# The second layer of a routed expert block by one level of Strassen's scheme, in half-width column tiles

## The chip, the cores and the metric

The kernel runs on one core of one Trainium2 chip. The metric is the device time of one execution in microseconds; before the change the median of three runs is 424.77 us (424.56 to 424.95). The profile is one further execution, with a span of 419.8 us. The five engines of a core are called here as in the profile: PE (TensorE, matrix products; PEld is its weight load), DVE (VectorE), ACT (ScalarE), POOL (GpSimd) and SP (SyncE, which issues most transfers).

## The reference, cut to what matters

Two stages. The first is a linear attention with a decaying state; it gives a matrix x of 3072 tokens by 384. The second sends each token to one of 8 experts. Everything is in 32-bit floats.

```python
# first stage, per batch and head
y[t]  = r[t] @ (state + outer(u * k[t], v[t]))
state = w[:, None] * state + outer(k[t], v[t])

# second stage: N = 3072 tokens, D = 384, E = 8 experts, F = 1024
logits     = x @ w_gate
expert_idx = argmax(logits, axis=1)
gate_w     = softmax(logits)[arange(N), expert_idx]
for e in range(E):
    mask = expert_idx == e
    h  = maximum(x[mask] @ w1[e], 0.0)      # first layer,  384 -> 1024
    ye = h @ w2[e]                          # second layer, 1024 -> 384
    out[mask] = gate_w[mask, None] * ye
```

## The kernel before

The attention half and the routing take about the first 157 us of the span. Then the tokens stand in tiles of 128, all of one expert, and a loop works through the tiles. Two tiles run ahead of the loop, the loop has 22. A tile gathers its tokens from HBM with an indirect transfer (`load_x`), transposes them (`turn`), and applies the first layer (`hidden`, in two halves of four blocks of 128 hidden units each) and the second layer (`result`). Which expert a tile has is only known at run time, so instructions that read the weights `w2_all` take an index from a register.

```python
def turn(self, mo, tag, copy=nc.vector.tensor_copy):
    p = self.R.ps.tile([128, DT, 128], FP32, name="xTp", tag=tag, bufs=BUFS[tag])
    for d in range(DT):                                   # DT = 3
        nc.tensor.transpose(p[:, d, :], self.xs[:, 128 * d:128 * d + 128], ident)
    self.xT = self.tile(mo, [128, DT, 128], "xT", 2)
    copy(self.xT, p)

def hidden(self, mo, fb):
    if fb == 0:
        self.hT = self.tile(mo, [128, FT, 128], "hT", 2)  # FT = 8
    p = self.R.ps.tile([128, 4, 128], FP32, name="hp", tag=f"P{fb}", bufs=2)
    for f in range(4):
        q, o = 2 * fb + f // 2, f % 2 * 128
        for d in range(DT):
            nc.tensor.matmul(p[:, f, :], lhsT=self.w1[:, q, d, o:o + 128], rhs=self.xT[:, d, :],
                             start=d == 0, stop=d == DT - 1)                      # L1045
    nc.scalar.activation(self.hT[:, 4 * fb:4 * fb + 4, :], p, func=ACT.Relu)      # L1047

def result(self, mo, within=None):
    p = self.R.ps.tile([128, DM], FP32, name="yp", tag="y", bufs=2)               # DM = 384
    e = slice(self.j, self.j + 1) if self.early else ds(self.expert(ENG.PE), 1)
    for f in range(FT):
        # ... cut: work of the next tile that one early tile puts in here
        rhs = w2_all[:, e, f * DM:(f + 1) * DM]
        nc.tensor.matmul(p, lhsT=self.hT[:, f, :], rhs=rhs, start=f == 0, stop=f == FT - 1)  # L1056
    self.y = self.tile(mo, [128, DM], "yo", 3)
    nc.vector.tensor_scalar_mul(self.y, p, self.xs[:, DM:W])                      # L1058
```

The loop (`tiles` are the 22; `seg` is one tile more that holds the remainders of four experts, 32 tokens each, whose work is spread over the loop in eight odd tiles):

```python
for j, t in enumerate(tiles):
    i = (j - 5) // 2 if j % 2 and 5 <= j < 5 + 4 * FQ else None    # FQ = 4
    if j + 2 < len(tiles):
        tiles[j + 2].load_x(mo)
    # ... cut
    t.hidden(mo, 0)
    if i is not None:
        if i < FQ:
            seg.quarter(mo, i)      # hg: 12 products in column tiles of 32
        else:
            seg.add(i - FQ)         # yg: 8 products in column tiles of 32
        if i + 2 < 2 * FQ:
            seg.load(mo, i + 2)
    t.hidden(mo, 1)
    if i is not None and i < FQ:
        seg.turn_quarter(i)         # hgT: two transposes
    if j + 2 < len(tiles):
        tiles[j + 2].load_w1(wp)
    # ... cut
    if j + 1 < len(tiles):
        tiles[j + 1].turn(mo, "g")
    # ... cut
    t.result(mo)
    t.store()
    # ... cut
```

The attention half holds instructions whose durations are of use here: pairs of products that write the two halves of 64 partitions (column tiles), lines L599 and L603, and elementwise products on GpSimd (L514, L515, L520) and VectorE (L510).

Of the kernel before, what the change touches and what calls it, by code (L numbers as in the profile page):

```python
# [10 lines left out]
FP32 = mybir.dt.float32  # L11
# [3 lines left out]
ALU = mybir.AluOpType  # L15
ACT = mybir.ActivationFunctionType
PSUM = bass.MemoryType.PSUM
ENG = mybir.EngineType

B, H, S, D = 4, 8, 768, 48  # L20
E, F = 8, 1024
DM = H * D
# [7 lines left out]
DT = DM // 128  # L30
FT = F // 128
WLO, WHI = 0.6, 1.6
W = DM + 1
SEG = 32
NS = 4
# [3 lines left out]
FQ = 4  # L39
FW = F // FQ  # L40
# [13 lines left out]
def rwkv5_then_switch(ctx, tc, r, k, v, rk, tok, wu_in, wg, wgh, w1, w2, out):  # L54
# [8 lines left out]
    nc = tc.nc  # L63
# [6 lines left out]
    w2_all = consts.tile([128, E, FT * DM], FP32, name="w2_all")  # L70
# [62 lines left out]
    with tc.manual_schedule():  # L133
# [10 lines left out]
        for l in range(LV):  # L144
            n = 1 << l
# [279 lines left out]
    def fast():  # L425
# [242 lines left out]
        for i, load in enumerate(pieces[AHEAD:]):  # L668
            piece.setdefault(turns[i * len(turns) // n], []).append(load)

        with tc.manual_schedule():
# [4 lines left out]
            for load in pieces[:AHEAD]:  # L676
                load()
# [18 lines left out]
            for u in range(NU):  # L696
# [4 lines left out]
                for load in piece.get(u, ()):  # L701
                    load()
# [53 lines left out]
            for step in R.onehots(B - 1):  # L756
# [13 lines left out]
            t1.store()  # L770
            late = late_tiles_of(R, NSURE - NEARLY)
            run_tiles(tiles[2:], wp, mo, Segments(R, 0), zip(late, [xbs[1][:, i] for i in range(G)] + [t0.xs, t1.xs],
                                                             strict=True))
        em.close()
# [213 lines left out]
    class Tile:  # L988
# [47 lines left out]
        def hidden(self, mo, fb):  # L1036


            if fb == 0:
                self.hT = self.tile(mo, [128, FT, 128], "hT", 2)  # L1040
            p = self.R.ps.tile([128, 4, 128], FP32, name="hp", tag=f"P{fb}", bufs=2)
            for f in range(4):
                q, o = 2 * fb + f // 2, f % 2 * 128
# [6 lines that stand above are left out]
            p = self.R.ps.tile([128, DM], FP32, name="yp", tag="y", bufs=2)  # L1050
            e = slice(self.j, self.j + 1) if self.early else ds(self.expert(ENG.PE), 1)
            for f in range(FT):
                if within and f == FT - 2:
                    within()
                rhs = w2_all[:, e, f * DM:(f + 1) * DM]
                nc.tensor.matmul(p, lhsT=self.hT[:, f, :], rhs=rhs, start=f == 0, stop=f == FT - 1)  # L1056
            self.y = self.tile(mo, [128, DM], "yo", 3)
            nc.vector.tensor_scalar_mul(self.y, p, self.xs[:, DM:W])  # L1058

        def store(self):  # L1060
            s_ = nc.gpsimd.indirect_dma_start(  # L1061
                out=out[:, :], out_offset=bass.IndirectOffsetOnAxis(ap=self.idx, axis=0),
                in_=self.y[:, :], in_offset=None, bounds_check=N - 1, oob_is_err=False)
            tc.declare_no_dep(s_.ins, group="sc", reason="each token stands in one tile: the rows are disjoint")
            tc.add_to_no_dep_group("sc", s_.ins)

    class Segments(Tile):
# [9 lines left out]
        def load(self, mo, i):  # L1077

            q = i % FQ
            if i == 0:  # L1080
                self.es = [self.expert(ENG.SP, NTILE + self.j * NS + k) for k in range(NS)]
                self.w = {}
            self.w[i] = self.tile(mo, [128, NS, DT * FW], "wq", 2)
            for k, e in enumerate(self.es):
                src = w1[ds(e, 1), q].rearrange("a p d f -> p (a d f)") if i < FQ else \
                    w2[ds(e, 1), q].rearrange("a p f -> p (a f)")
                nc.sync.dma_start(self.w[i][:, k], src)
# [26 lines left out]
        def add(self, q):  # L1114

            if q == 0:
                self.p = self.R.ps.tile([128, DM], FP32, name="yg", tag="rw", bufs=1)
            n = FT // FQ
            for f in range(n):
                for i in range(NS):  # L1120
                    t = slice(SEG * i, SEG * i + SEG)
                    nc.tensor.matmul(self.p[t, :], lhsT=self.hT[:, n * q + f, t],  # L1122
                                     rhs=self.w[FQ + q][:, i, f * DM:(f + 1) * DM], start=q == 0 and f == 0,
                                     stop=q == FQ - 1 and f == n - 1, skip_group_check=True)
# [5 lines left out]
    def run_tiles(tiles, wp, mo, seg, late):  # L1130


        for j, t in enumerate(tiles):
            i = (j - 5) // 2 if j % 2 and 5 <= j < 5 + 4 * FQ else None
            if j + 2 < len(tiles):
                tiles[j + 2].load_x(mo)
            if j == 2:
                seg.load_x(mo)
            t.hidden(mo, 0)
            if i is not None:  # L1140
                if i < FQ:
                    seg.quarter(mo, i)
                else:
                    seg.add(i - FQ)
                if i + 2 < 2 * FQ:
                    seg.load(mo, i + 2)
            t.hidden(mo, 1)
            if i is not None and i < FQ:
                seg.turn_quarter(i)
            if j + 2 < len(tiles):  # L1150
                tiles[j + 2].load_w1(wp)
            if j in (2, 3):
                seg.load(mo, j - 2)
            if j + 1 < len(tiles):
                tiles[j + 1].turn(mo, "g")
            if j == 4:
                seg.turn(mo, "rw")
            t.result(mo)
            t.store()
            if j >= 6:  # L1160
                for x, xs in islice(late, 1):
                    x.load_x(xs)
            if i == 2 * FQ - 1:
                seg.result(mo)
                seg.store()
# [31 lines left out]
    def after_general():  # L1197
        es, em = ExitStack(), ExitStack()
        ps = es.enter_context(tc.tile_pool(name="pm", bufs=1, space=PSUM))
        rt = es.enter_context(tc.tile_pool(name="rt", bufs=1))  # L1200
        mo = em.enter_context(tc.tile_pool(name="mo", bufs=2))
        R = Routes(ps, rt, 0)
        R.begin()
        for b in range(B):
            for step in R.ranks(b, "rw") + R.onehots(b):
                step()
        R.bases(rt)
        R.order(rt)
        R.owners(rt, NSURE)
        R.slots(rt)  # L1210
        R.index(rt, "rw")
        tiles = [Tile(R, j) for j in range(NSURE)]
        with tc.manual_schedule():
            for i in range(2):
                tiles[i].load_w1(mo)
                tiles[i].load_x(mo)
            tiles[0].turn(mo, "g")
            xl = rt.tile([128, NTILE - NSURE + E // NS - 1, W], FP32, name="xl")
            late = late_tiles_of(R, NSURE)
            run_tiles(tiles, mo, mo, Segments(R, 0), zip(late, [xl[:, i] for i in range(len(late))], strict=True))  # L1220
        em.close()
        late_tiles(R, late)
        es.close()
# [65 lines left out]
```

## Time and profile before

| | |
|---|---|
| median time | 424.77 us |
| span of the profiled execution | 419.8 us |
| PE busy, share of the span | 403.8 us, 96% |
| DVE, ACT, POOL busy | 153.2, 127.4, 150.2 us |
| granted PE clock, mean | 0.992 |
| first layer L1045, second layer L1056, share of the chain that ended last | 29%, 27% |
| transfers | 99.00 MB, mean 236 GB/s |

The page gives, for each engine, its busy time and how that lies over 40 slices of the span (a digit is tenths of a slice). The chain that ended last is found by going back from the last instruction, at each step to what released it. A timeline lists instructions in order of time; a run of equal instructions is merged into one row with its count. One 32-bit matrix product appears as two MATMUL and two LDWEIGHTS records, so counts of records are twice those of the code. In a timeline an instruction's releaser stands in brackets behind the idle time before it.

### The profile page before, as it was taken

To read this page: it belongs to the slowest core of one execution; us is meant where nothing else is said; L and a number is where in the kernel's file an instruction comes from. 1 tells how busy PE (TensorE), PEld (TensorE's weight loads), DVE (VectorE), ACT (ScalarE), POOL (GpSimd) and SP (SyncE) were. 2 spreads that over 40 slices of the span, in tenths; PEclk is the share of its full clock that TensorE was granted. 3 is DMA by queue.
4 is the path that set the end of the run, shared out by engine and by line. 5 is a ranking of instruction groups with operands and counts; after the bars stand their busy time and mean duration, and the time that the engine had idled before them with its cause. 6 is when DMAs were issued, how large, how long until landed. Compare 5 with 4: busy or idle time off the path is not lost.

```text
span 419.8 us, 10366 instructions
## 1 busy us (share of the span) xinstructions
PE 403.8 (96%) x4057; PEld 333.6 (79%) x4057; DVE 153.2 (36%) x409; ACT 127.4 (30%) x395; POOL 150.2 (36%) x192
## 2 busy tenths in 40 slices
PE   7999999999999979999999999999999999999990
PEld 7899999998999757788888777777878776776770
DVE  6887899999875910011111011110111011110100
ACT  4787777776773221111111011011111011011110
POOL 6998769569750021121111222122222111110100
PEclk9999999999999999999999999999999999999996
DMA  7989999999992999558866585976867675455000
GB/s 254 255 236 275 282 276 304 263 285 263 280 286 106 348 336 356 180 194 323 322 197 236 203 322 204 302 241 225 283 220 260 230 289 187 165 174 187 33 23 27
DMA packets 42944, 99.00 MB, mean 236 GB/s; under 512 B 5189, under 2 KB 16474, under 8 KB 42882
## 3 DMA queue, kind: packets, MB, share of 16 engines
q1 hardware_dynamic: 39024, 86.94, 63.7%
q0 software_dynamic: 3712, 11.23, 8.5%
q8 instruction: 37, 0.61, 0.7%
q14 instruction: 25, 0.20, 0.2%
q10 hardware_dynamic: 146, 0.01, 0.0%
HBM read 88.72 MB, written 9.65 MB: 234 GB/s over the span
## 4 chain that ended last, share of the span: by engine, by line
PE 86%; DVE 6%; ACT 2%; DMA 2%; POOL 1%; issue 1%; POOLq 0%; DVEq 0%
PE hp L1045 29%; PE yp L1056 27%; PE P L532 5%; PE P L542 5%; PE yp L603 5%; PE yp L599 4%; PE rp L634 4%; PE Gp L578 2%; PE xTp L1032 2%; DMA xs<-x_hbm,idx 1%; PE hg L1102 1%; PE yg L1122 1%; ACT A L553 1%; DVE At L842 1%; DVE A L564 1%
## 5 line engine op out<-in xcount | busy, mean ns | idle before, releaser
L1045 PEld LDWEIGHTS hp<-xT,w1s 128*128 128x128 f32 x1152 | 133.1, 192 | 10.4 <-issue 4.1
L1045 PE MATMUL hp<-xT,w1s 128*128 128x128 f32 x1152 | 135.2, 276 | 0.0
L1056 PE MATMUL yp<-w_all,hT 128*128 (+1 forms) x384 | 128.0, 486 | 0.0
L1056 PEld LDWEIGHTS yp<-w_all,hT 128*128 128x128 f32 x384 | 71.0, 190 | 44.3
L1047 ACT ACTIVATE hT<-hp 128x512 f32<-128x512 f32 x48 | 28.7, 598 | 225.5 <-PE hp L1045 185.4
L1061 POOL DMA_INDIRECT out_dram<-yo,idx x22 | 22.3, 1013 | 191.9 <-DVE yo L1058 182.4
L553 ACT ACTIVATE A<-ident,dv 128x128 f32<-128x128 f32 x192 | 59.7, 389 | 0.2 <-ACT dv L550 0.2
L1058 DVE TENSOR_SCALAR yo<-yp,xs 128x384 f32<-128x384 f32 x22 | 13.6, 618 | 106.5 <-PE yp L1056 106.5
L1034 DVE COPY xT<-xTp 128x384 f32<-128x384 f32 x23 | 12.8, 556 | 100.2 <-PE xTp L1032 100.2
L603 PE MATMUL yp<-A,w_all 128*64 128x128 f32 x384 | 39.7, 275 | 0.2
L514 POOL TENSOR_TENSOR w_all<-w_all 128x384 f32<-128x384 f32 x30 | 31.0, 1035 | 21.9 <-DMA w_all<-in_r_k_units_dram 5.4
L564 DVE COPY_PREDICATED A<-mask,P 128x384 f32<-128x384 int32 x64 | 36.2, 588 | 5.8 <-ACT A L553 5.2
L1026 POOL DMA_INDIRECT xs<-x_hbm,idx x22 | 21.3, 968 | 33.0 <-ACT idxs L986 26.6
L599 PE MATMUL yp<-w_all,St 128*64 128x128 f32 x320 | 32.6, 275 | 0.0
L515 POOL TENSOR_TENSOR w_all<-w_all,W 128x384 f32<-128x384 f32 x30 | 31.4, 1046 | 0.0
L542 PE MATMUL P<-w_all 48*128 48x128 f32 x384 | 29.5, 286 | 0.5 <-ACT dv L550 0.5
L532 PEld LDWEIGHTS P<-wu,w_all 48*128 48x128 f32 x384 | 23.9, 187 | 4.3 <-issue 1.9
L532 PE MATMUL P<-wu,w_all 48*128 48x1 f32 x384 | 26.7, 250 | 0.2 <-POOL St L449 0.2
L603 PEld LDWEIGHTS yp<-A,w_all 128*64 128x64 f32 x384 | 25.8, 137 | 1.3 <-DVE A L564 1.1
L520 POOL TENSOR_TENSOR Kg<-w_all,Wg 128x288 f32<-128x288 f32 (+1 forms) x32 | 25.5, 798 | 2.7 <-DVE Wg L474 2.1
L510 DVE TENSOR_TENSOR w_all<-w_all,W 128x384 f32<-128x384 f32 x30 | 25.9, 865 | 0.3 <-DMA w_all<-in_r_k_units_dram 0.3
L542 PEld LDWEIGHTS P<-w_all 48*128 48x128 f32 x384 | 24.2, 188 | 0.6 <-ACT dv L550 0.6
(167 smaller groups left out, 292.0 us busy)
## 6 DMA issues: line engine op xcount, KB each, us to landing
w1s<-in_moe_w_dram SPq DMA_DIRECT2D x22, 1536.0 KB
wq<-in_moe_w_dram SPq DMA_DIRECT2D x32, 384.0 KB
w_all<-in_v_k_units_dram SPq DMA_DIRECT2D x64, 144.0 KB
w_all<-in_r_k_units_dram SPq DMA_DIRECT2D x56, 144.0 KB
w_all<-in_moe_w_dram SPq DMA_DIRECT2D x20, 384.0 KB
w_all<-in_moe_w_dram SPq DMA_DIRECT2D x3, 1536.0 KB
x_hbm<-xb SPq DMA_DIRECT2D x9, 385.0 KB
w1s<-in_moe_w_dram SPq DMA_DIRECT2D x8, 384.0 KB
```

The lines of the kernel that those rows point to most:

```text
L510: nc.vector.tensor_tensor(x["R"], x["r"], bc(W1[:, x["hp"], None, :], [128, HC, C]), op=ALU.mult)
L514: nc.gpsimd.tensor_tensor(x["RK"], x["r"], x["k"], op=ALU.mult)
L515: nc.gpsimd.tensor_tensor(x["K"], x["k"], bc(W2[:, x["hp"], None, :], [128, HC, C]), op=ALU.mult)
L532: nc.tensor.matmul(P[hi][:, o:o + 1], lhsT=x["RK"][q, c, :], rhs=wu[q, 1, hp:hp + 1], start=True, stop=True, skip_group_check=True)
L542: nc.tensor.matmul(P[hi][:, c * C:(c + 1) * C], lhsT=x["K"][q, c, :], rhs=x["R"][q, c, :], start=True, stop=True, skip_group_check=True)
L553: nc.scalar.activation(A[:, hi, c, :], ident, func=ACT.Copy, scale=dv[:, hi, c:c + 1])
L564: nc.vector.copy_predicated(A[:, hi], bc(mask[:, None, :].bitcast(I32), [128, HC, C]), P[hi][:, 0:HC * C].rearrange("p (c t) -> p c t", t=C))
L599: nc.tensor.matmul(yp[q, c, :], lhsT=old[:, hi, :], rhs=x["R"][:, c, :], start=True, stop=False, skip_group_check=True)
L603: nc.tensor.matmul(yp[q, c, :], lhsT=vh(x, c, hi, 64), rhs=x["A"][:, hi, c, :], start=old is None, stop=True, skip_group_check=True)
L1045: nc.tensor.matmul(p[:, f, :], lhsT=self.w1[:, q, d, o:o + 128], rhs=self.xT[:, d, :], start=d == 0, stop=d == DT - 1)
L1047: nc.scalar.activation(self.hT[:, 4 * fb:4 * fb + 4, :], p, func=ACT.Relu)
L1056: nc.tensor.matmul(p, lhsT=self.hT[:, f, :], rhs=rhs, start=f == 0, stop=f == FT - 1)
```

## The change

Strassen's scheme multiplies two 2 x 2 block matrices with seven block products in place of eight, at the price of sums of blocks before and after. Here the tile's 128 tokens are cut into halves i of 64, the 1024 hidden units into halves of 512 (four blocks of 128 each), and the 384 output columns into halves of 192. A block product is then four products of a 64-column stationary operand with 192 moving columns. Since an output half has 64 tokens, it fills only half of the array's columns: two block products run side by side, one to partitions 0 to 63 and one to 64 to 127. The seventh is cut in two by its hidden units, and the two partial sums lie in the two halves. So there are 14 pairs of half products in place of 8 full ones, for 21 of the 22 tiles of the loop; the last tile and the two ahead of the loop keep `result`.

Sums of weight blocks (`T`, four) are formed for each tile anew, two on GpSimd and two on VectorE; sums of activation blocks (`S`, four) on VectorE; the seven products are put together by one ACT copy, eight VectorE adds and a scaling on ACT. To make room, `hT` and the segment weights `wq` have one buffer in place of two, and the segment loads stand later.

```diff
             if fb == 0:
-                self.hT = self.tile(mo, [128, FT, 128], "hT", 2)
+                self.hT = self.tile(mo, [128, FT, 128], "hT", 1)
...
+        def sums_w(self, mo, eng):
+            e = ds(self.expert(ENG.Pool if eng is nc.gpsimd else ENG.DVE), 1)
+            b = lambda i, k: w2_all[:, e].rearrange(
+                "p a (i f k d) -> p (a i) f k d", i=2, f=FT // 2, k=2)[:, i, :, k]
+            sub = lambda *a: eng.tensor_tensor(*a, op=ALU.subtract)
+            if eng is nc.gpsimd:
+                T = self.T = self.tile(mo, [128, 4, FT // 2, DM // 2], "T", 1)
+                sub(T[:, 3], b(1, 1), b(0, 1))
+                sub(T[:, 0], b(0, 1), b(0, 0))
+            else:
+                T = self.T
+                sub(T[:, 1], b(1, 1), T[:, 0])
+                sub(T[:, 2], b(1, 0), T[:, 1])
+
+        def sums_h(self, mo, fb):
+            a = lambda i, j: self.hT[:, FT // 2 * j:FT // 2 * j + FT // 2, 64 * i:64 * i + 64]
+            if fb == 0:
+                S_ = self.S = self.tile(mo, [128, 4, FT // 2, 64], "S", 1)
+                nc.vector.tensor_tensor(S_[:, 3], a(0, 0), a(1, 0), op=ALU.subtract)
+            else:
+                S_ = self.S
+                nc.vector.tensor_tensor(S_[:, 0], a(1, 0), a(1, 1), op=ALU.add)
+                nc.vector.tensor_tensor(S_[:, 1], S_[:, 0], a(0, 0), op=ALU.subtract)
+                nc.vector.tensor_tensor(S_[:, 2], a(0, 1), S_[:, 1], op=ALU.subtract)
+
+        def products(self):
...          # a, b, s, t: blocks of hT, w2, S, T
+            self.p = [self.R.ps.tile([128, 2, DM // 2], FP32, name=f"m{i}", tag="y", bufs=2) for i in range(2)]
+            def product(i, k, *halves):
+                for f in range(n):                                   # n = 4
+                    for hi, (x, y) in enumerate(halves):
+                        nc.tensor.matmul(self.p[i][64 * hi:64 * hi + 64, k, :], lhsT=x(f), rhs=y(f),
+                                         start=f == 0, stop=f == n - 1, skip_group_check=True)
+            product(0, 0, (a(0, 0), b(0, 0)), (a(1, 1), t(2)))
+            product(0, 1, (a(0, 1), b(1, 0)), (s(3), t(3)))
+            product(1, 0, (s(2), b(1, 1)), (s(0), t(0)))
+            for f in range(n // 2):
+                for hi in range(2):
+                    g = f + n // 2 * hi
+                    nc.tensor.matmul(self.p[1][64 * hi:64 * hi + 64, 1, :], lhsT=s(1)(g), rhs=t(1)(g),
+                                     start=f == 0, stop=f == n // 2 - 1, skip_group_check=True)
+
+        def combine(self, mo):
+            lo, up, k = slice(0, 64), slice(64, 128), DM // 2
+            p, q = self.p
+            u = self.tile(mo, [128, 3, k], "u", 1)
+            y = self.y = self.tile(mo, [128, DM], "yo", 3)
+            add = lambda *a: nc.vector.tensor_tensor(*a, op=ALU.add)
+            nc.scalar.copy(u[lo, 0], p[lo, 0])
+            add(y[lo, 0:k], p[lo, 1], u[lo, 0])
+            add(u[lo, 1], q[lo, 1], u[lo, 0])
+            add(u[lo, 1], q[up, 1], u[lo, 1])
+            add(u[up, 2], p[up, 1], u[lo, 1])
+            add(u[lo, 2], q[lo, 0], u[lo, 1])
+            add(y[up, 0:k], p[up, 0], u[up, 2])
+            add(y[up, k:], q[up, 0], u[up, 2])
+            add(y[lo, k:], q[up, 0], u[lo, 2])
+            nc.scalar.activation(y, y, func=ACT.Copy, scale=self.xs[:, DM:W])
...
-            self.w[i] = self.tile(mo, [128, NS, DT * FW], "wq", 2)
+            self.w[i] = self.tile(mo, [128, NS, DT * FW], "wq", 1)
...
     def run_tiles(tiles, wp, mo, seg, late):
+        for eng in (nc.gpsimd, nc.vector):
+            tiles[0].sums_w(mo, eng)
         for j, t in enumerate(tiles):
...
+            fast = j < len(tiles) - 1
             t.hidden(mo, 0)
+            if fast:
+                t.sums_h(mo, 0)
...
-                if i + 2 < 2 * FQ:
-                    seg.load(mo, i + 2)
+                if i + 1 < 2 * FQ:
+                    seg.load(mo, i + 1)
             t.hidden(mo, 1)
+            if fast:
+                t.sums_h(mo, 1)
...
-            if j in (2, 3):
-                seg.load(mo, j - 2)
+            if j == 3:
+                seg.load(mo, 0)
...
-            t.result(mo)
+            if fast:
+                t.products()
+                if j + 2 < len(tiles):
+                    tiles[j + 1].sums_w(mo, nc.gpsimd)
+                t.combine(mo)
+                if j + 2 < len(tiles):
+                    tiles[j + 1].sums_w(mo, nc.vector)
+            else:
+                t.result(mo)
             t.store()
```

More of the change, by code (lines that the diff above doesn't have):

```diff
@@ new lines, in products @@
+        def products(self):
+            e, n = ds(self.expert(ENG.PE), 1), FT // 2
+            S_, T, hT = self.S, self.T, self.hT
+            a = lambda i, j: lambda f: hT[:, n * j + f, 64 * i:64 * i + 64]
+            b = lambda i, k: lambda f: w2_all[:, e, (n * i + f) * DM + k * (DM // 2):(n * i + f) * DM + (k + 1) * (DM // 2)]
+            s = lambda i: lambda f: S_[:, i, f, :]
+            t = lambda i: lambda f: T[:, i, f, :]
+            self.p = [self.R.ps.tile([128, 2, DM // 2], FP32, name=f"m{i}", tag="y", bufs=2) for i in range(2)]
[12 more added lines that the diff above has]
+                                     start=f == 0, stop=f == n // 2 - 1, skip_group_check=True)
```

## The prediction, made before the changed kernel ran

> **What bounds the kernel now.** I read the page first: the busy time by engine, then the slices.
>
> ```profile
> PE 403.8 (96%) x4057; PEld 333.6 (79%) x4057; DVE 153.2 (36%) x409; ACT 127.4 (30%) x395; POOL 150.2 (36%) x192
> ...
> PE   7999999999999979999999999999999999999990
> ...
> DVE  6887899999875910011111011110111011110100
> ```
>
> TensorE is full; in the second half of the span VectorE is nearly idle. That half is the loop over 22 tiles which the change touches. Next I read the chain that ended last, in order of time (start, length, what; a 32-bit product counts as two records):
>
> ```profile
> 223.92 5.36 PE hp L1045 x48
> 229.28 0.33 PE xTp L1032 x3
> 229.60 5.16 PE yp L1056 x16
> 234.77 2.68 PE hp L1045 x24
> 237.44 1.43 PE hg L1102 x24
> 238.88 2.88 PE hp L1045 x24
> ```
>
> From 157 us to the end the chain never leaves TensorE: nothing else delays it. One tile costs 5.36 (first layer, 24 products of 128 columns: 0.223 each) + 0.33 (three transposes) + 5.16 (second layer, 8 products of 384 columns: 0.645 each) = 10.85 us. So what the change does to the time is what it does to TensorE's own work plus every new wait of TensorE, and there is no slack in which such a wait could hide.
>
> Two products give a line: (645 - 223) / 256 = 1.65 ns per column, with about 12 ns fixed.
>
> **What the Trainium skill says.** (1) "TensorEngine Tiling (Array Packing)", Key Properties: different tiles of the array run matmuls in parallel, but a change of the tiling mode drains TensorE. The first part agrees with the attention half of this trace, where pairs of 64-column tiles run (timeline of TensorE: start, length):
>
> ```profile
> 120.52 0.40 PE L599 MATMUL yp<-w_all,St 128*64 128x128 f32 x4
> 120.75 0.39 PE L603 MATMUL yp<-A,w_all 128*64 128x128 f32 x4
> 120.97 0.39 PE L599 MATMUL yp<-w_all,St 128*64 128x128 f32 x4
> ```
>
> Starts are 0.22 us apart for a pair of products of 128 columns, what one full product of 128 costs (0.223): pairs overlap fully, also in L603, where the halves stream different data. The second part shows in the chain above: hg is three groups of four 32-column tiles, 256 moving columns each, so 3 x (0.223 + 128 x 0.00165) = 1.30 us; it takes 1.43. The hp half behind it takes 2.88 instead of 2.68. A trip into column tiles and out again costs 0.13 + 0.20 us here. (2) "VectorE: DVE Perf Modes", The perf-mode tier table: a 32-bit tensor_tensor has only the 1x rate. The trace agrees: 407 ns for 256 elements and 546 for 384 (lines L148, L503), 1.08 ns per element. (3) "SBUF — State Buffer", Who interferes with whom: a VectorE instruction with two SBUF inputs and a GpSimd instruction that reads SBUF exclude each other. The trace agrees: L510, a product of two SBUF tiles, has a least time of 544 and a median of 908 ns beside GpSimd work. In the new loop the two rarely meet: the recombination reads one input from PSUM, and VectorE's sums of the weights wait for GpSimd's anyway.
>
> **The change part by part**
>
> *Arithmetic.* The 8 products of 384 columns (5.16 us) become 28 half products of 64 x 192 in 14 pairs. A pair of 192 columns should take 0.219 + 64 x 0.00165 = 0.325 us; 14 x 0.325 = 4.55 us. Gain 0.61 us per tile; over the 21 tiles that use it 12.8 us, or 3%. This is the purpose, and the ceiling.
>
> *Mode switch.* The loop now enters and leaves column tiles once more per tile: 0.33 us by the measurement above, of which the 0.20 of leaving stays in every case.
>
> *The wait on the second half of hT.* This is the step that the diff hides. The old second layer ran f = 0..7, so the half of hT that comes last was first needed 4 x 0.645 = 2.58 us after its start. The new first pair is (a00, b00) beside (a11, T2), and a11 is rows from f = 4: the second instruction needs it at once. The timeline of a plain tile shows when it is ready:
>
> ```profile
> 223.76 5.52 PE L1045 MATMUL hp<-xT,w1s 128*128 128x128 f32 x48
> 223.96 0.62 DVE L1058 TENSOR_SCALAR yo<-yp,xs 128x384 f32<-128x384 f32 x1 [4.60 <-PE yp L1056]
> ...
> 229.11 0.49 PE L1032 MATMUL xTp<-ident,xs 128*128 128x128 f32 x3
> ...
> 229.31 0.60 ACT L1047 ACTIVATE hT<-hp 128x512 f32<-128x512 f32 x1 [2.02 <-PE hp L1045]
> 229.33 0.62 PEld L1056 LDWEIGHTS yp<-w_all,hT 128*128 128x128 f32 x3
> 229.44 0.81 PE L1056 MATMUL yp<-w_all,hT 128*128 x2
> ```
>
> TensorE begins the second layer at 229.44, but ScalarE's Relu ends at 229.91. With 0.05 for the signal and 0.11 from weight load to product (229.33 to 229.44), the lower half of the array starts at 230.07, 0.63 us late. The upper half can run only its one product (0.33) ahead, since the queue is in order. So: 230.07 + 4.55 + 0.20 for leaving = 234.82, where the next first layer began at 234.60 before (229.44 + 5.16). **Per plain tile +0.2 us**: gain 0.61, wait 0.63, leaving 0.20; the entry lies inside the wait. In the 4 tiles that also transpose the shared hidden tile (hgT, 0.22 us more before the second layer), the old start was 218.59 and Relu ended at 218.85: 218.85 + 0.16 + 4.55 + 0.20 = 223.76, exactly the old 218.59 + 5.16. **+0.0 there.**
>
> *The sums of the weights T, on GpSimd then VectorE.* One buffer: GpSimd may start only when the products of the tile before are done. Lines L520 and L514 have least times of 584 and 994 ns for 192 and 384 elements, 2.14 ns per element: 768 elements 1.82 us. Two back to back, 0.20 after the last product (the lag of L1058 behind yp above): ready at +3.8. VectorE's two, dependent: 546 + 384 x 1.08 = 0.96 us each with some 0.06 of signal: ready at +5.85. Recombination stands before them on VectorE: seven adds of 192 after the last product, about 0.35 each (the L1112 and L1034 copies from PSUM, 425 ns for 256 and 556 for 384, give 0.36 for 192), with signals 2.8 us, over at +3.0, before GpSimd is. TensorE asks for T2 at 0.20 (leaving) + 5.68 (223.76 to 229.44) + 0.63 = +6.5. Slack 0.5 us with no loader tile, 2 with one. **No cost in the steady state**, by a small margin.
>
> *The first tile.* T cannot be built a tile ahead: GpSimd's queue has the second early tile's store first (timeline, L1061 at 157.59, over at 158.6). Then 158.9 + 3.6 = 162.5, + 2.0 = 164.5 for T2, + 0.16 = 164.7 for the product. Old start of that second layer in the same count: 167.35 - 5.16 = 162.19. End 164.7 + 4.55 + 0.20 = 169.45 against 167.35: **+2.1 us, once.**
>
> *Sums of the activations S.* Four adds of 256, 0.41 each; the last three follow Relu, ready about 1.4 us after it; first asked for after two products, 8 x 0.325 = 2.6 us. Hidden. *ScalarE*: copy and scale about 0.9 us per tile, beside 1.2 before. Hidden. *Single buffers of hT and wq*: the next Relu comes 2.7 us after the old readers end; the segment weights have two tiles (23 us) to arrive at some 230 GB/s, 1.5 MB needing 7. Hidden. *Last tile*: old code, same tail.
>
> **Sum.** 21 tiles: 1 first at +2.1, 16 plain at +0.2 = 3.2, 4 with hgT at 0: +5.3 us. 424.8 + 5.3 = **430 us**, 1.3% slower.
>
> **The rivals.** *A: the ceiling is reached.* If Relu's lag cost nothing and switching were free, 424.8 - 12.8 = 412. Against it: the wait stands in the instruction order, and the two times 229.44 and 229.91 are measured. If only leaving were free, plain tiles come out level: 427. *B: T becomes the bound.* The chain GpSimd, GpSimd, VectorE, VectorE has 0.5 us of slack. If GpSimd needs 2.4 us instead of 1.8 for these strided blocks, or recombination takes over 3.6 us, T2 is late in each of the 12 tiles after the first that have no loader work; 0.7 us late would be +8: 438. For it: L515 also has instances up to 1322 ns beside VectorE. Against it: those meet two-SBUF-input work, which is not there at that time. *C: column pairs run slower than 0.325*, because each pair needs four weight loads and mostly one address instruction where there was one per 0.645. The 0.22 pairs of L603 show that loads alone fit; the address instructions are untested. 20 ns more per pair would be 14 x 21 x 0.02 = +6: 436.
>
> **Range and chances.** The ceiling of 3% is eaten almost wholly by two measured things, so faster by over 2% (under 416.3) would need both of them wrong: 0.03. B and C push up only; one of them in part is quite possible, and slower by over 2% starts at 433.3: 0.27. The rest, 0.70, within 2%. Range 423 to 438.
>
> **What would show it.** In the profile after, MATMULs of the products should start 0.325 apart by pairs, and the block from its first product to the next hp should be near 5.4 us rather than 5.16. TensorE's largest new wait should be on ScalarE (hT), some 0.3 to 0.5 us in each of 17 tiles; if it names VectorE (T) instead, B holds. The first block should wait some 2 us for T. GpSimd's sums should be near 1.8 us, VectorE's T sums near 0.96. The prediction is wrong downward if the pair of the first product does not wait, wrong upward if T2 ends later than 6.5 us after the last product.

## The result, and the profile after

The changed kernel takes 427.59 us (median of 4 runs, 426.89 to 428.51) against 424.86 us for the kernel before beside it: a ratio of 1.0064, 95% interval 1.0043 to 1.0086. A second series gave 1.0107 (1.0076 to 1.0139). An eighth of the second layer's products is gone, and the kernel is about 1% slower.

The page, the busy time by engine and three lines of the slices:

```profile
PE 408.9 (96%) x4897; PEld 368.5 (86%) x4897; DVE 270.5 (63%) x682; ACT 144.8 (34%) x437; POOL 244.2 (57%) x234
...
PE   7999999999999979999999999999999999999990
...
DVE  6887899869885914666656656566656556564620
...
POOL 6996769769650025575554556466765645454500
```

VectorE and GpSimd have become busy in the second half, by 117 and 94 us. TensorE is still full, so neither has become the bound. The reading must come from TensorE's own time, tile by tile. The chain of the kernel after, for one plain tile (start, length, what; L1102 and L1111 are the products):

```profile
178.15 4.31 PE m L1102 x47
182.46 0.10 PE m L1111
182.63 0.65 PE m L1111 x7
183.28 5.55 PE hp L1045 x48
188.83 0.33 PE xTp L1032 x3
189.16 4.31 PE m L1102 x47
```

From 178.15 to 189.16 are 11.01 us, where a plain tile took 10.85. The second layer takes 183.28 - 178.15 = 5.13 us instead of 5.16, hardly less; the first layer behind it takes 5.55 instead of 5.36, with the same instructions, to which the experiments come back. What the second layer loses shows in the timeline at one change of layers (start, length, engine, line; the idle time before it and its releaser in brackets):

```profile
188.67 0.49 PE L1032 MATMUL xTp<-ident,xs 128*128 128x128 f32 x3
...
188.87 0.60 ACT L1047 ACTIVATE hT<-hp 128x512 f32<-128x512 f32 x1 [1.84 <-PE hp L1045]
188.90 0.42 DVE L1083 TENSOR_TENSOR S<-hT 128x256 f32<-128x256 f32 x1
189.09 0.19 PEld L1102 LDWEIGHTS m<-w_all,hT 128*64 128x64 f32 x2 [0.17 <-issue]
...
189.52 0.19 PEld L1102 LDWEIGHTS m<-T,hT 128*64 128x64 f32 x2 [0.24 <-ACT hT L1047]
...
190.06 0.33 PE L1102 MATMUL m<-T,hT 128*64 128x192 f32 x1
...
190.22 0.33 PE L1102 MATMUL m<-T,hT 128*64 128x192 f32 x1
...
190.38 0.33 PE L1102 MATMUL m<-T,hT 128*64 128x192 f32 x1
```

The prediction calls the half of the array that writes partitions 0 to 63 the upper one (`lo` in the code), the other the lower one. The first product of the upper half starts at 189.09. The first of the lower half, which reads the last half of hT, starts only at 189.52, just after ScalarE's Relu ends at 189.47. For these 0.43 us the lower half stands still, and the upper half runs one product and no more: its second starts at 189.63. After that each half starts a record every 0.16 us, so a product (two records) every 0.325. The pairs run as fast as they should.

The profiled execution of the changed kernel has a span 7.0 us longer than that of the kernel before, because it also lost some 2 us ahead of the loop, and because the granted TensorE clock was 0.5 from 157.4 to 160.8 us, where the kernel before has 1.0 (1.7 us, in an early tile's second layer and the first layer after it). The comparison of plain tiles leaves that out; the loop's first tile is touched by it, as is said further below.

### The profile page after: what moved, and what is told of

It is laid out like the page before. It is cut to its first block, busy times and chain, and to the rows that moved or that the text cites. A ratio compares the mean times of both kernels' runs of the same rounds, so it can differ in the third digit from the quotient of the medians.

```text
span 426.8 us, 12759 instructions
## 1 busy us (share of the span) xinstructions
PE 408.9 (96%) x4897; PEld 368.5 (86%) x4897; DVE 270.5 (63%) x682; ACT 144.8 (34%) x437; POOL 244.2 (57%) x234
## 4 chain that ended last, share of the span: by engine, by line
PE 90%; issue 2%; POOL 2%; DMA 1%; SPq 1%; ACT 1%; DVE 1%; POOLq 0%
PE hp L1045 30%; PE m L1102 21%; PE P L542 6%; PE P L532 5%; PE yp L603 5%; PE yp L599 4%; PE rp L634 4%; PE m L1111 4%; PE Gp L578 3%; PE yp L1056 2%; PE xTp L1032 2%; PE hg L1173 1%; PE yg L1193 1%; DMA w_all<-in_r_k_units_dram 1%; POOL T L1068 1%
## 5 line engine op out<-in xcount | busy, mean ns | idle before, releaser
L1068 POOL TENSOR_TENSOR T<-w_all 128x768 f32 x42 | 75.3, 1813 | 86.6 <-issue 81.4
L1102 PE MATMUL m<-w_all,hT 128*64 x336 | 62.4, 331 | 0.0
L1068 DVE TENSOR_TENSOR T<-w_all,T 128x768 f32<-128x768 f32 x42 | 40.2, 958 | 28.7 <-POOL T L1068 28.0
L1102 PE MATMUL m<-T,S 128*64 128x192 f32 x336 | 58.0, 326 | 0.0
L1119 DVE TENSOR_TENSOR u<-m,u 64x192 f32<-64x192 f32 x84 | 29.8, 355 | 27.4 <-PE m L1111 25.3
L1102 PEld LDWEIGHTS m<-T,S 128*64 128x64 f32 x336 | 46.0, 137 | 0.0
L1102 PEld LDWEIGHTS m<-w_all,hT 128*64 128x64 f32 x336 | 42.7, 136 | 3.8 <-issue 3.5
L1119 DVE TENSOR_TENSOR yo<-m,u 64x192 f32<-64x192 f32 x84 | 28.2, 356 | 27.3 <-ACT u L1120 26.0
L1102 PE MATMUL m<-T,hT 128*64 128x192 f32 x168 | 31.8, 332 | 1.0 <-DVE T L1068 1.0
L1102 PE MATMUL m<-w_all,S 128*64 x168 | 30.7, 326 | 0.0
```

What stands on the lines that cost most here:

```text
L1068: sub = lambda *a: eng.tensor_tensor(*a, op=ALU.subtract)
L1102: nc.tensor.matmul(self.p[i][64 * hi:64 * hi + 64, k, :], lhsT=x(f), rhs=y(f), start=f == 0, stop=f == n - 1, skip_group_check=True)
L1119: add = lambda *a: nc.vector.tensor_tensor(*a, op=ALU.add)
```

## The experiments

The measure here is the tile: the time from the first transpose to the first transpose one tile later, in the trace; it holds one second layer and the first layer behind it. In every kernel below, tiles of one kind agree within 0.02 us unless said (tiles behind hgT, tiles with the shared tile's products and the first tile are other kinds), so hundredths can be read where whole runs scatter by several microseconds.

| kernel | plain tile, us | tiles 2 to 20 together, us | whole run against the kernel before (95%) |
|---|---|---|---|
| before | 10.85 | 220.3 | 1 |
| after | 11.01 | 222.1 | 1.0064 (1.0043 to 1.0086) |
| after, second series | 11.00 | 222.1 | 1.0107 (1.0076 to 1.0139) |
| late half first, on before | 11.47 | 231.0 | 1.0281 (1.0207 to 1.0355) |
| column tiles, on before | 11.19 | 226.9 | 1.0233 (1.0153 to 1.0313) |
| order of pairs and of s3 | 10.58 | 215.3 | 0.9873 (0.9811 to 0.9935) |
| order of pairs only | 10.94 | 218.9 | 1.0059 (1.0030 to 1.0088) |
| sums of weights left out | 11.01 | 224.8 | 1.0147 (1.0093 to 1.0201) |
| shared trip, on the reordered kernel | 10.58 | 214.0 | 0.9872 (0.9809 to 0.9935) |
| first layer in column tiles, on the reordered kernel | 10.42 | 211.8 | 0.9802 (0.9726 to 0.9878) |
| all together | 10.42 | 211.8 | 0.9803 (0.9748 to 0.9858) |

### The wait alone: the late half of hT first, in the kernel before

```diff
-            for f in range(FT):
+            for i in range(FT):
+                f = (i + FT // 2) % FT
```

(with `start` and `stop` on i; the same eight products.)

> The kernel before, with the eight products of the second layer in the order f = 4..7, 0..3, so that the half of hT that comes last is needed first; same work. Theory (the lag from the last first-layer product to the Relu result costs TensorE 0.5 us where nothing stands between): 18 loop tiles at +0.5, 4 with hgT at +0.3: +10 us, about 435 us, with TensorE waiting for ScalarE hT in each. Rival (Relu is in time, or the wait is absorbed by the queue): 425 us.

Measured: 435.46 us against 423.80, and 11.47 us per plain tile: +0.62. Timeline of a change of layers in this kernel:

```profile
185.60 0.49 PE L1032 MATMUL xTp<-ident,xs 128*128 128x128 f32 x3
...
185.80 0.60 ACT L1047 ACTIVATE hT<-hp 128x512 f32<-128x512 f32 x1 [2.02 <-PE hp L1045]
...
186.45 0.62 PEld L1057 LDWEIGHTS yp<-w_all,hT 128*128 128x128 f32 x3 [0.60 <-ACT hT L1047]
```

The transposes' product starts at 185.60, the second layer at 186.45, 0.85 later where it was 0.33: +0.52, waiting for ScalarE. The other 0.10 lies inside the block, whose 5.16 became 5.26; its cause is open. No Strassen and no column tile is in this kernel, so the lag of Relu alone can cost as much as the scheme saves.

### The trip into column tiles alone, in the kernel before

```diff
-                nc.tensor.matmul(p, lhsT=self.hT[:, f, :], rhs=rhs, start=f == 0, stop=f == FT - 1)
+                for hi in range(2):
+                    q = slice(64 * hi, 64 * hi + 64)
+                    nc.tensor.matmul(p[q, :], lhsT=self.hT[:, f, q],
+                                     rhs=w2_all[:, 0:1, f * DM:(f + 1) * DM] if hi else rhs, ...)
```

> The kernel before, with its second layer as two column tiles of 64 tokens for each product of 128, same moving columns, no Strassen; the upper half reads the weights of expert 0 in every tile,[...] so this kernel computes something else for these rows. The arithmetic time is the same (two concurrent products of 384 columns, 0.645 us). Theory (going into column tiles and out costs about 0.33 us each time): 24 tiles x 0.33 = +8 us, about 433 us; the first layer after it reads 5.46 instead of 5.36, the step from transposes to the second layer 0.42 instead of 0.33, the block itself 5.29 instead of 5.16. Rival (the loss in the changed kernel comes from the small weight loads and the waits, switching is free): 425 us.

Measured: 433.87 us against 423.80, +0.34 per plain tile. The chain of this kernel:

```profile
175.93 5.31 PE yp L1058 x32
181.24 5.55 PE hp L1045 x48
186.80 0.33 PE xTp L1032 x3
```

The block takes 5.31 for 5.16 (+0.15) and the first layer after it 5.55 for 5.36 (+0.19): the same 5.55 as in the changed kernel. (Counted from start to start of the records, as the expectation counts, the three steps are 0.42, 5.31 and 5.46; the "upper half" of the expectation is partitions 64 to 127.) So that part of the loss comes with the column tiles, and with nothing of Strassen's sums.

### The order of the pairs, in the changed kernel

```diff
-            product(0, 0, (a(0, 0), b(0, 0)), (a(1, 1), t(2)))
-            product(0, 1, (a(0, 1), b(1, 0)), (s(3), t(3)))
+            product(0, 0, (a(0, 0), b(0, 0)), (s(3), t(3)))
+            product(0, 1, (a(0, 1), b(1, 0)), (a(1, 1), t(2)))
...   # combine() reads p[up, 0] and p[up, 1] the other way round
             if fast:
                 t.sums_h(mo, 0)
+                t.sums_w(mo, nc.vector)      # behind s3; before, it stood behind combine()
```

> The changed kernel with the products in another order: the first pair is (a00, b00) beside (s3, t3), which needs only the first half of hT, and (a11, t2) moves to the second pair; VectorE forms s3 before its two sums of weights. Theory (the wait on the second half of hT eats the gain): in the trace of the changed kernel the second product of a plain tile starts 0.43 us after the first. That goes: a plain tile falls from 11.00 to about 10.57 us, the four tiles with hgT by some 0.2, the first tile's wait for T2 by about 1.4. 16 x 0.43 + 4 x 0.2 + 1.4 = 9 us less: about 418.5 us, 1.5% under the kernel before. Rival (the loss is the change of tiling mode and the rate of the pairs, and the wait only hides entry costs that come back): 425.5 to 427.5 us.

Measured: 416.93 us against 423.80. The chain:

```profile
184.19 0.33 PE xTp L1032 x3
184.51 4.05 PE m L1102 x48
188.56 0.65 PE m L1111 x8
189.21 5.55 PE hp L1045 x48
```

The block is 4.70 us instead of 5.13, and no product waits any more; 10.58 per plain tile, to be held against 10.57 foretold. The 0.43 us was the wait. The whole run is 1.3% under the kernel before, where 1.5% had been foretold. The first layer stays at 5.55, as it should if that part belongs to the shape. The block is 0.15 over the 4.55 of its 14 pairs, as the block of 8 pairs above was 0.15 over 5.16: this part is paid once per block and not per pair.

### The order of the pairs without moving s3

> The changed kernel with only the order of the products altered; VectorE still forms its two sums of weights before s3. In the trace of the changed kernel s3 ended 0.23 us after the first product of the tile began (189.32 against 189.09). Theory (the first pair then waits on s3, because VectorE's sums of weights stand before it): a plain tile takes about 10.8 us, half way between 11.00 and 10.58; the first tile's wait for T stays in part. About 422 us for a kernel before of 424.8. Rival (the order of the products alone did it, s3 is early enough): 10.58 us per plain tile.

Measured: 424.74 us against 422.85, 0.6% over the kernel before where about 0.7% under it had been foretold, and a split picture. The second layer of a plain tile takes 0.36 us more than with both edits (10.94 per tile); that of a loader tile, which has 1.4 us more TensorE work ahead of it and so finds s3 done, takes what it takes with both (10.58). Timeline of this kernel:

```profile
183.30 1.95 DVE L1068 TENSOR_TENSOR T<-w_all,T 128x768 f32<-128x768 f32 x2 [1.15 <-POOL T L1068]
...
185.17 0.42 DVE L1083 TENSOR_TENSOR S<-hT 128x256 f32<-128x256 f32 x1
...
185.34 0.19 PEld L1102 LDWEIGHTS m<-w_all,hT 128*64 128x64 f32 x2 [0.17 <-issue]
...
185.70 0.19 PEld L1102 LDWEIGHTS m<-T,S 128*64 128x64 f32 x2 [0.17 <-issue]
```

s3 starts at 185.17, in the place behind the sums of weights, and ends at 185.59; the pair had been free to start at 185.34. The view names only "issue" for this wait, but the times leave s3. A better order on TensorE is worth little until the engine that feeds it has the same order.

### The sums of weights left out

```diff
                 if j + 2 < len(tiles):
-                    tiles[j + 1].sums_w(mo, nc.gpsimd)
+                    tiles[j + 1].T = t.T
...   # and no sums_w on VectorE behind combine()
```

> The changed kernel, with the sums of weights formed for the first tile of the loop only and used in all (it leaves out these sums for 20 tiles, and so computes with the wrong weights there). GpSimd loses 73 us of work and VectorE 38. Theory (sums of weights are hidden in the steady state): within 1 us of the changed kernel, 427 to 428 us; the wait of the first tile stays. Rival (T is the bound, or its traffic slows the other engines): 3 us or more faster, under 424.5 us.

Measured: 429.76 us against 423.80, not faster than the changed kernel but some 2 us over what was foretold. Tiles take what they take there (11.01, 12.85, 12.63), except four, all with the second layer of a loader tile, that take 11.46 to 11.64 where the changed kernel has 10.79 to 11.01: 2.7 us together. In those, ScalarE's Relu starts late:

```profile
241.81 1.02 POOL L1132 DMA_INDIRECT out_dram<-yo,idx  x1 [8.71 <-ACT yo L1129]
...
246.16 0.60 ACT L1047 ACTIVATE hT<-hp 128x512 f32<-128x512 f32 x1 [2.61 <-PE xTp L1032]
```

The profile puts its start down to the transposes and not, as elsewhere, to the first layer; why it is held so long only there stays open. For the question asked the answer is plain: removing 73 us of GpSimd and 38 of VectorE work takes nothing off a tile. The sums of weights are hidden.

### The changed kernel once more

> The changed kernel once more, beside the variants on the same chip: about 0.6% over the kernel before, plain tiles 11.00 us. If its gap to the reordered kernel is again 8 to 9 us, the gap is the order's; if it has moved, the comparison across chips is not to be trusted at this size.

Measured: 427.44 us against 422.85, 1.1% over the kernel before where 0.6% was expected, but 11.00 us per plain tile, as the first time. The kernel of the next section, which holds the reordering, ran beside it at 417.46, 10.0 us less; its tiles put 1.3 us of that down to a second edit. The gap between the orders is there again, and the tiles agree in both series.

### Where a trip can be saved

Two edits, each on the reordered kernel. The first puts the shared tile's products (hg, yg) directly behind the second layer, and their two transposes one tile later:

> The reordered kernel (first pair from the first half of hT), and in the eight loader tiles the shared tile's products in 32-column tiles (hg, yg) stand directly behind the second layer instead of in the middle of the first, their two transposes one tile later. Theory (each trip into column tiles costs 0.33 us, and one trip serves both): eight trips less, at most 8 x 0.33 = 2.6 us under the reordered kernel, and some 0.1 per tile less of that if going from 64 to 32 columns costs too: 1.6 to 2.6 us less, about 1.7% under the kernel before. Rival (the cost belongs to each first instruction of a new shape, whatever stands before it): no change against the reordered kernel, 1.3% under the kernel before.

Measured: 417.46 us against 422.85. Tiles 2 to 20 take 1.3 us less than in the reordered kernel; but for one loader tile that is 0.27 longer than its like it would be 1.6, or 0.20 per loader tile. A trip costs 0.34, so the step from 64 to 32 columns keeps 0.14 of it. The 1.3 us lie under the range foretold (1.6 to 2.6); only with that one tile set aside does its lower edge hold. Why that tile is longer is open.

The second puts the first layer into column tiles as well, two of 64 hidden units each:

```diff
-                    nc.tensor.matmul(p[:, f, :], lhsT=self.w1[:, q, d, o:o + 128], rhs=self.xT[:, d, :], ...)
+                    for hi in range(2):
+                        nc.tensor.matmul(p[64 * hi:64 * hi + 64, f, :],
+                                         lhsT=self.w1[:, q, d, o + 64 * hi:o + 64 * hi + 64], rhs=self.xT[:, d, :], ...)
```

> The reordered kernel with the first layer too in two column tiles of 64, its arithmetic time the same (0.219 us for a pair of 128 columns where the full product takes 0.223). TensorE then leaves column tiles only for the three transposes of a tile. Theory (the cost is the round trip, whatever lies on either side): still one round trip per tile, now around the transposes; a plain tile at 10.5 us against 10.58, by the slightly faster pairs alone, and in the loader tiles no trip more for hg and yg apart from 64 to 32 columns. Rival (the cost of leaving belongs to the first layer's long run of full products): the first layer gets back its 0.1 and more, a plain tile at 10.3.

Measured: 414.77 us against 422.85, 10.42 per plain tile, between what the theory (10.5) and the rival (10.3) gave. The chain:

```profile
183.81 0.48 PE xTp L1032 x3
184.29 4.05 PE m L1103 x48
188.34 0.65 PE m L1112 x8
188.99 5.24 PE hp L1046 x96
```

A trip remains, now round the transposes: they take 0.48 for 0.33 (+0.15), and the products still 4.70 (+0.15 over 4.55). The first layer takes 5.24, close to the 24 x 0.219 = 5.26 of its pairs, and no longer carries 0.19 of a trip. So the trip fell only from 0.34 to 0.30, and 0.12 of the 0.16 gained per plain tile is the rate of the pairs. Neither view was right alone: the cost is mainly the round trip, as the theory has it, but what stands on either side sets some of it. How, is not settled.

### All together

> The reordered kernel with the first layer in column tiles, the shared tile's products behind the second layer, and GpSimd's sums of weights for the first tile of the loop put ahead of the second early tile's store. Theory (three separate costs, each measured: the trips round hg and yg, 0.1 to 0.2 in eight tiles now that the first layer is in column tiles too; the first tile's wait on T, whose block took 5.88 us where the others take 4.60 in the kernel with the first layer in column tiles): 1 and 1.2 us less than that kernel, which stood at 0.980 of the kernel before: about 0.975. Rival (the gains overlap, and the first tile's wait goes to the arrival of the last weights instead): 0.979 to 0.980.

Measured: 414.42 us against 422.41, the same 0.980: the rival's number held. Loader tiles take 12.28 us as without the shared trip; that fits a count of two changes of shape round the 32-column products wherever they stand, now that the first layer is in 64-column tiles, but is not shown apart. The first tile's block fell from 5.88 to 5.27, but not to 4.60. GpSimd, put ahead of the store, starts its sums 3.82 us after the transposes before that tile's first layer (159.89 against 156.07) where it was 4.41 (158.88 against 154.47). In the kernel without that edit the trace names the arrival of the last weights as what released GpSimd there, and not the store; in the kernel with it, it names only "issue". So what holds the sums, and what gave the 0.6 us, is open.

## Why the prediction was right

**The sum.** For a plain tile three terms explain the measured change to a hundredth: 10.85 - 0.61 (arithmetic) + 0.34 (trip) + 0.43 (wait) = 11.01. The arithmetic is 14 times the measured rate of the pairs; the trip is measured apart by column tiles in the kernel before, the wait by reordering the pairs. With only the trip left, a tile is 10.58 = 10.85 - 0.61 + 0.34.

**The rate of the pairs.** 0.325 us foretold from pairs of 128 columns and the slope of two full products; 0.325 in the trace. Rival C (loads and address instructions slow the pairs) is out.

**The trip.** Foretold as 0.13 + 0.20 from hg; 0.15 + 0.19 measured. That "TensorEngine Tiling (Array Packing)", Key Properties, says a change of the tiling mode drains TensorE fits; the page gives no size, which was in this trace only. No run here shows the drain itself.

**The wait.** Found in the right place, and a little too large: 0.63 us foretold from the old start of the second layer to the first lower product, 0.52 measured (189.52 against 188.67 + 0.33). The 0.11 between weight load and product that the prediction added is not paid after a wait: both records stand at 189.52. From there to the next transposes the trace has 10.15 us (199.67 - 189.52), 0.04 more than the 4.55 + 0.20 + 5.36 of the prediction, so the entry did not lie wholly inside the wait. The prediction therefore gave +0.22 (written +0.2) per plain tile where +0.16 was measured, and 0.0 behind hgT where it is -0.06. The tile that also transposes the shared tokens gains too (12.85 us for 13.02); the prediction counted it as plain.

**T.** Foretold to arrive 0.5 us before it is asked for, with GpSimd's sums at 1.82 us and VectorE's at 0.96. The groups of the kernel after:

```profile
L1068 POOL TENSOR_TENSOR T<-w_all 128x768 f32 x42 | 75.3, 1813 | 86.6 <-issue 81.4
...
L1068 DVE TENSOR_TENSOR T<-w_all,T 128x768 f32<-128x768 f32 x42 | 40.2, 958 | 28.7 <-POOL T L1068 28.0
...
L1119 DVE TENSOR_TENSOR u<-m,u 64x192 f32<-64x192 f32 x84 | 29.8, 355 | 27.4 <-PE m L1111 25.3
```

1.813, 0.958 and 0.355 us. T2 is ready at 187.03 + 1.95 = 188.98, 0.54 before the lower product at 189.52. Rival B is out, by this and by the kernel without the sums.

**The first tile.** +2.1 us were foretold, and +1.2 measured in the profiled execution (12.09 us for the tile), +0.9 in that of the second series (11.72). The mechanism is the one named:

```profile
161.80 3.61 POOL L1068 TENSOR_TENSOR T<-w_all 128x768 f32 x2
...
165.44 1.95 DVE L1068 TENSOR_TENSOR T<-w_all,T 128x768 f32<-128x768 f32 x2 [4.93 <-POOL T L1068]
...
165.57 0.49 PE L1032 MATMUL xTp<-ident,xs 128*128 128x128 f32 x3
...
167.54 0.35 PE L1102 MATMUL m<-T,hT 128*64 128x192 f32 x1 [1.00 <-DVE T L1068]
```

In both executions, though, the granted clock was 0.5 for 3.4 us just before (157.4 to 160.8, and 158.0 to 161.4). So the first layer ahead of this tile ran longer, 5.92 and 6.29 us where the prediction had taken 5.36, and that gave T time. The kernel with only the order of the pairs changed forms T at the same place in the program, and its trace has a clock of 1.0 there and a first layer of 5.36:

```profile
160.71 0.49 PE L1032 MATMUL xTp<-ident,xs 128*128 128x128 f32 x3
...
161.43 1.95 DVE L1068 TENSOR_TENSOR T<-w_all,T 128x768 f32<-128x768 f32 x2 [5.26 <-POOL T L1068]
```

T2 is ready at 163.38, 2.67 us after the transposes begin; the prediction had 164.5 - 161.85 = 2.65, and the changed kernel at the lowered clock 1.82. So the term that looks too large by 0.9 us was sized well for an execution without that stretch, and the +1.2 owes something to chance. Why the clock fell there in these executions is open.

**The total.** 430 us stood for 424.8 + 5.3. Measured by tiles the loop lost 1.8 (tiles 2 to 20) + 1.2 (first tile) = 3.0 us; with the first tile at its foretold +2.1 it would be 3.9, an estimate from these two numbers. The medians differ by 2.7 us in the first series and by 4.6 in the second, on either side of it, so their nearness to 3.0 or to 5.3 is no finer check than that; the tiles are. Rival A, the ceiling of 412, was rightly ruled out: even with the wait gone the trip takes 0.34 of each 0.61.

## What to carry to other kernels

When an operation that streams is reordered, look up when each operand is first asked for: the old loop gave Relu 2.6 us of grace merely by its order, and the new one took it away. Smaller matrix work on a full engine has to be weighed against every change of tile shape; here a trip of 0.34 us eats more than half of an eighth of 5.16. Then put the operands that come first into the first products, and give the engine that makes them the same order: that turned about +1% into -1.3%; column tiles for the first layer too brought -2%.

## What the runs showed of the hardware that was not expected

GpSimd's indirect store took 1.01 us in the kernel before and takes 1.65 in the mean after. It is long where it stands beside VectorE's two sums of weights, as here in the kernel after:

```profile
187.03 1.95 DVE L1068 TENSOR_TENSOR T<-w_all,T 128x768 f32<-128x768 f32 x2 [1.14 <-POOL T L1068]
187.16 1.71 POOL L1132 DMA_INDIRECT out_dram<-yo,idx  x1 [0.16 <-ACT hT L1047]
```

In the kernel without these sums the same store took 1.02 us (shown above). In the kernel after, all 21 indirect transfers of GpSimd that begin in the loop while these two sums run take 1.70 to 1.74 us; the 53 of the kernel before from 155 us on take 0.95 to 1.03. The Trainium skill, "SBUF — State Buffer", Who interferes with whom, infers that a tensor_tensor does not hold up the making of descriptors, since it takes only the read interface of the shared pair; these runs show a store beside it that is 0.7 us longer. No product waits for that store, so it costs nothing in a plain tile.
